# Dense chunks of 512 tokens, with columns 0-263 of the second product behind all logits and a list schedule for the front of the kernel

## The chip, the cores and the metric

One core of a Trainium2 chip runs the kernel. The engines are TensorE (PE, with its weight loads shown as PEld), VectorE (DVE), ScalarE (ACT), GpSimd (POOL) and SyncE (SP, which here only issues DMAs). The metric is device time in microseconds (us) of one launch, as the median of several runs.

## The reference

Three stages run one after another, all in float32 precision.

1. Sparse attention: q, k, v of 4 batches x 8 heads x 576 positions x 64. Heads 0 to 3 look at the last 32 positions, heads 4 to 7 at the earlier positions of the same residue class modulo 32:

```python
scores = np.where(masks[None], scale * q @ k.T, -1e9)
attn = exp(scores - max); attn = attn / (sum(attn) + 1e-09)
x = (attn @ v)                    # 2304 tokens x 512
```

2. A dense feed-forward: `h = x @ w_in` (512 to 2048), `g = h * sigmoid(h)`, `x = g @ w_out` (2048 to 512). These two weights come as 64-bit floats.

3. A mixture of 8 experts with a greedy global assignment: `logits = x @ w_gate`, all 18,432 logits sorted from the top, and each token goes to the first expert that still has one of its 288 places. Then `out[mask] = relu(x[mask] @ w1[e]) @ w2[e]` for each expert e (512 to 1024 to 512).

## The kernel before

**Arithmetic.** Every product of the dense and the expert stage is done as three fp32r matmuls: each operand is split into a high part (an ACT copy, rounded) and a low part (DVE: source minus high part), and high x high, high x low and low x high are summed in PSUM.

**Front.** `attention` works in pairs of heads, 16 in all, 4 for each batch; a pair has two halves with `scores` (PE, then DVE maximum, ACT exponentials), `norm` (DVE or POOL), `turn` (PE transposes, ACT copies), and then `values` (PE, ACT and DVE copies into the tile xf of the batch). The 64-bit weights arrive as raw words. `pieces` (lines 610, 613, 616) rebuilds float32 from them with three DVE operations for 512 elements, and its second part (lines 625, 626) splits them. `gate_turn` and `gate_columns` fold the router's `w_gate` into `w_out`: for every two blocks of w_out, 8 transposes (line 641), two ACT copies and 16 small matmuls (line 656) give 8 more columns, so that the second product delivers the logits too.

**Dense stage.** The tokens are 9 chunks of 256. A unit is a chunk and one of 8 pairs of 128-row blocks of the hidden layer. `gemm1` has 24 matmuls of 256 columns a unit (lines 693 to 695), `silu` two ACT and two DVE operations of 128x512. `gemm2` follows one unit behind. Its output columns are in two parts: A, columns 0-255 (line 746), and B, columns 256-511 with the 8 logits, 264 wide (line 749), each 12 matmuls a unit. Chunks 0 and 1 compute A and B at once; chunks 2 to 8 (`DEFER = 2`) compute B alone and store g, the high and low parts, to DRAM (tiles gd).

**Order.** The front is written out by hand: `START` names for each step of the first batch's attention what else is issued (C a conversion step, L a split, T and G gate steps, X a split of x, P a part of gemm1, R a load), and `BESIDE` does so for each half unit of chunks 0 and 1. A small list, `REST`, holds low parts back for a step. From the middle of chunk 1 on, `side` spreads the attention of batches 1 to 3 over the units of chunks 1 to 5. Engines run their queues in the order of issue; so does SP with its DMAs.

**Behind the logits.** `Router.phase` finds one expert's tokens at a time (DVE with small PE products). Meanwhile PE does the put-off A columns of chunks 2 to 8, with g read back into six buffers gk (`RELOADS`), the router's products in between by `tick` and `hop`, a running estimate of the time. Then x of the first expert is gathered, and 8 experts run in `ffn_a` and `ffn_b`, while the router goes on and the expert weights are loaded and split.

Of the kernel before, what the change touches and what calls it, by code (L numbers as in the profile page):

```python
# [23 lines left out]
NE = 8  # L24
# [21 lines left out]
DEFER = 2  # L46
RELOADS = 6

START = (
    "", "", "", "", "", "", "", "", "C0 C0 C1 C0 Rs2", "Ro1", "L0 C1 C1 C2", "C2", "L1 C2 C3", "C3 Ri3",
    "C3 L3", "", "", "L2", "X0 X2", "C4 X1", "C4 C4 C5 T1 C5 P10", "C6 L4 C5 P00 P11", "X3",
)
BESIDE = (
# [4 lines left out]
)  # L62
SPARE_SB = 2
FIRST_LOADS = "e q0 v0 q2 q1 i01 v2 o01 i00 o00 v1 i10 q3 v3 i11"
# [6 lines left out]
CLOSED = 1.0e6  # L71

# [291 lines left out]
def kernel(  # L364
# [22 lines left out]
    gdr = {(c, fp): dram.tile([128, 2, 512], F, name=f"gd{c}_{fp}") for c in range(DEFER, NCHUNK) for fp in range(NFP)  # L387
           if c <= LATE or fp < 2}
# [15 lines left out]
    xsp = pool(ctx, name="xsp", bufs=4, side="right")  # L404
    st_xf, st_bat, st_ps, st_c = (ctx.enter_context(ExitStack()) for _ in range(4))
# [3 lines left out]
    pacc = pool(st_ps, name="pacc", bufs=1, space=PSUM)  # L409
# [24 lines left out]

    REST = []

    def rest(what, f, src=False):
        REST.append([what, f, 0, src])

    def settle(what=None, src=False):  # L440

        for r in list(REST):
            if src and r[3] or what is not None and what == r[0] or (
                    what is None and not src and r[2] > 0):
                REST.remove(r)
                r[1]()
            else:
                r[2] += what is None and not src

    def new_sb():  # L450
        settle()
        if sum(r[3] for r in REST) > SPARE_SB:
            settle(src=True)
        return ap.tile([128, 512], F, name="sb", bufs=7)


    def scores(n, half):
        if half == 0 and NPAIR < n + 1 < NP:
            load_qk(n + 1)
# [23 lines left out]
        sb = new_sb()  # L483
# [8 lines left out]
        nc.vector.tensor_scalar(mx[:, :units], mx[:, :units], -1.0 / math.sqrt(D), None, op0=OP.mult)  # L492
        sm = ap.tile([128, 5], F, name="sm")
# [5 lines left out]
    def norm(n, half):  # L499
        sv, sm = PR[n, half]  # L500
        units = 5 if half == 0 else 4
        nc.vector.tensor_scalar(sm[:, :units], sm[:, :units], 1e-9, None, op0=OP.add)
        nc.vector.reciprocal(sm[:, :units], sm[:, :units])
        if (n, half) in NORM_ON_POOL:
            nc.gpsimd.tensor_tensor(sv, sv, sm[:, :units, None].to_broadcast([128, units, WIN[n % NPAIR]]), op=OP.mult)
        else:
            for u in range(units):
                nc.vector.tensor_scalar(sv[:, u, :], sv[:, u, :], sm[:, u:u + 1], None, op0=OP.mult)

    def turn(n, half):  # L510
# [3 lines left out]
        for u in range(4):  # L514
            nc.tensor.transpose(pt[:W, 128 * u:128 * u + 128], sv[:, u, :], ident)
        t = ap.tile([96, 512], F, name="ptA" if half == 0 else "ptB", bufs=1)
        nc.scalar.activation(t[:W], pt[:W], AF.Copy)
        PT[n, half] = t
        if half == 0:
            pt = patt.tile([128, 512], F, name="att")  # L520
            nc.tensor.transpose(pt[:W, :128], sv[:, 4, :], ident)
            t = ap.tile([96, 128], F, name="ptM", bufs=1)
            nc.scalar.activation(t[:W], pt[:W, :128], AF.Copy)
            PT[n, 2] = t

    def values(n):
        b, pr = divmod(n, NPAIR)
        W = WIN[pr]
        if pr == 0:
            XF[b] = xfp.tile([128, NPAIR, S], F, name="xf")  # L530
        x = XF[b][:, pr, :]
        v = VW.pop(n)
        av = patt.tile([128, 512], F, name="att")
        for j in range(8):
            for a in range(2):
                mm(av[64 * a:64 * a + 64, 64 * j:64 * j + 64], v[:W, j, 64 * a:64 * a + 64],
                   PT[n, a][:W, 64 * j:64 * j + 64], start=True, stop=True)
        if pr < 2:
            nc.scalar.activation(x[:, :512], av, AF.Copy)
        else:  # L540
            xs = x.rearrange("p (i r) -> p r i", r=STRIDE)
            nc.scalar.activation(xs[:, 0:28, :], av[:, :504].rearrange("p (r i) -> p r i", i=NCLS), AF.Copy)
            nc.vector.tensor_copy(xs[:, 28, 0:8], av[:, 504:512])
        av = patt.tile([128, 512], F, name="att")
        for a in range(2):
            mm(av[64 * a:64 * a + 64, 0:64], v[:W, 8, 64 * a:64 * a + 64],
               PT[n, 2][:W, 64 * a:64 * a + 64], start=True, stop=True)
        if pr < 2:
            nc.vector.tensor_copy(x[:, 512:576], av[:, :64])
        else:  # L550
            nc.vector.tensor_copy(xs[:, 28, 8:18], av[:, 0:10])
            nc.vector.tensor_copy(xs[:, 29:32, :], av[:, 10:64].rearrange("p (r i) -> p r i", i=NCLS))
        if NPAIR < n + 1 < NP:
            load_v(n + 1)

    def attention(n0, n1):

        for k in range(2 * n0, 2 * n1 + 3):
            if k < 2 * n1:
                scores(*divmod(k, 2))  # L560
                yield
            if k >= 2 * n0 + 4 and k % 2 == 0:
                values(k // 2 - 2)
                yield
            if 2 * n0 < k <= 2 * n1:
                norm(*divmod(k - 1, 2))
            if 2 * n0 + 2 <= k < 2 * n1 + 2:
                turn(*divmod(k - 2, 2))
# [3 lines left out]
    WI, WO, RAW, ST, WT2, LATER = {}, {}, {}, {}, {}, {}  # L572

    def alloc_w(kind, c):
        n, t = (512, "wa") if kind == "i" else (520, "wb")
        (WI if kind == "i" else WO)[c] = tuple(wpool.tile([128, 4, n], R, name=t) for _ in range(2))

    def load_raw(kind, c, h, tag):
# [4 lines left out]
        t = wpool.tile([128, 2, 1024], I32, name=tag)  # L583
        nc.sync.dma_start(t, src)
        for k in range(2):
            RAW[kind, c, 2 * h + k] = t[:, k].rearrange("p (f w) -> p f w", w=2)

    def load_spare(kind, c, p, t):
        if not wide:
            return  # L590
        t = t.bitcast(I32)[:, 0:1024]
        nc.sync.dma_start(t, (w_in if kind == "i" else w_out)[c, p].bitcast(I32))
        RAW[kind, c, p] = t.rearrange("p (f w) -> p f w", w=2)

    def pieces(kind, c, p):

        if kind == "i" and p == 0 and c:
            alloc_w("i", c)
        if kind == "o" and p == 0 and c:
            alloc_w("o", c)  # L600
        sts = [new_sb() for _ in range(2)]
        if not wide:
            for i in range(2):
                nc.sync.dma_start(sts[i], (w_in if kind == "i" else w_out)[c, p + i])
        else:
            r = [RAW.pop((kind, c, p + i)) for i in range(2)]
            d = [st.bitcast(I32) for st in sts]
            v = nc.vector
            for i in range(2):
                v.tensor_scalar(d[i], r[i][:, :, 1], 3, 0x3FFFFFFF, op0=OP.logical_shift_left, op1=OP.bitwise_and)  # L610
            yield
            for i in range(2):
                v.scalar_tensor_tensor(d[i], r[i][:, :, 1], -0x40000000, d[i], op0=OP.bitwise_and, op1=OP.bitwise_or)  # L613
            yield
            for i in range(2):
# [669 lines left out]
```

## Time and profile before

| | us |
|---|---|
| median of 3 runs | 851.85 (851.37 to 852.91) |
| the profiled execution | 850.23 |
| its span, first to last instruction | 848.5 |
| PE busy | 798.8 (94%) |
| DVE busy | 505.0 (60%) |
| ACT busy | 364.5 (43%) |
| POOL busy | 81.2 (10%) |
| PE's share of the chain that ended last | 76% |

The profile is of one execution. Busy time counts an instruction from start to end; matmuls are pipelined and overlap, so the pace of PE is read from the distance between starts and not from durations. PEclk is the clock that was granted to PE, as a share of 2.4 GHz. A DMA share of 1 means that all 16 DMA engines are busy.

### The profile page before, as it was taken

Reading aid. Unit: us, or ns where it says so; the run is one execution under the profiler, and the core shown is the slowest. Engines: PE = TensorE matmul, PEld = TensorE weight load, DVE = VectorE, ACT = ScalarE, POOL = GpSimd, SP = SyncE. Lnnn points to the kernel's source line nnn. Section 1 sums busy time; section 2 is a strip of 40 time slices with the busy share of each in tenths; the row PEclk is TensorE's granted clock in tenths of the full one; section 3 lists DMA queues with packets and bytes.
Section 4 is the critical chain, followed back from the end, with each engine's and each line's share of the span. In section 5 each row is a group of like instructions: output and inputs, shape, how many; then the busy total and the mean of one; then the engine's idle time right before and its main releaser. Section 6 shows DMA issues by size and latency. Waiting matters only on the chain.

```text
span 848.5 us, 19455 instructions
## 1 busy us (share of the span) xinstructions
PE 798.8 (94%) x7623; PEld 771.5 (91%) x7623; DVE 505.0 (60%) x1582; ACT 364.5 (43%) x933; POOL 81.2 (10%) x133
## 2 busy tenths in 40 slices
PE   4689889999999999999999998999999999999995
PEld 3579888999999999899999998899999999999995
DVE  2959965564554554433334377778787887874440
ACT  3454434554455544443323212102455465456541
POOL 0000000000000000000003000001120311133631
PEclk9999989999999999999999999999999999999998
DMA  9960231231444444323335279993555655565630
GB/s 325 362 246 1 77 110 34 78 109 55 171 150 155 152 146 142 129 105 137 131 131 195 91 229 344 372 324 121 158 171 161 183 159 170 153 184 163 212 108 28
DMA packets 56907, 137.32 MB, mean 162 GB/s; under 512 B 6768, under 2 KB 10352, under 8 KB 56816
## 3 DMA queue, kind: packets, MB, share of 16 engines
q1 hardware_dynamic: 48832, 121.39, 42.7%
q0 software_dynamic: 3232, 9.96, 3.8%
q10 hardware_dynamic: 4752, 4.73, 1.6%
q8 instruction: 59, 0.97, 0.5%
q14 instruction: 32, 0.26, 0.1%
HBM read 99.89 MB, written 36.18 MB: 160 GB/s over the span
## 4 chain that ended last, share of the span: by engine, by line
PE 76%; DVE 13%; DMA 4%; ACT 4%; issue 1%; POOL 1%; ACTq 0%; POOLq 0%; SPq 0%
PE accB L749 11%; PE ph L693 7%; PE ph L695 7%; PE ph L694 7%; PE accA L746 6%; PE pm L1116 4%; PE pm L1117 4%; PE pm L1118 4%; PE pm L1095 3%; PE pm L1096 3%; PE pm L1097 3%; PE ph L746 3%; DVE sb L613 2%; PE att L210 2%; PE att L477 2%; DVE sb L616 2%
## 5 line engine op out<-in xcount | busy, mean ns | idle before, releaser
L693 PE MATMUL ph<-xh,wa 128*128 128x256 f32 x576 | 166.9, 290 | 0.0
L695 PE MATMUL ph<-xh,wa 128*128 128x256 f32 x576 | 164.0, 285 | 2.5 <-DVE wa L626 2.5
L694 PE MATMUL ph<-xl,wa 128*128 128x256 f32 x576 | 163.8, 284 | 0.5 <-DVE xl L675 0.5
L749 PE MATMUL accB<-wb,g 128*128 128x264 f32 x792 | 133.5, 290 | 0.5 <-ACT x2e L768 0.4
L712 DVE SCALAR_TENSOR_TENSOR gf<-gf,ph 128x512 f32<-128x512 f32 x72 | 49.5, 687 | 125.8 <-ACT gf L711 125.5
L749 PEld LDWEIGHTS accB<-wb,g 128*128 128x128 f32 x792 | 114.8, 192 | 2.5 <-ACT x2e L768 1.5
L695 PEld LDWEIGHTS ph<-xh,wa 128*128 128x128 f32 x576 | 110.5, 192 | 2.7 <-DVE wa L626 2.7
L693 PEld LDWEIGHTS ph<-xh,wa 128*128 128x128 f32 x576 | 110.7, 192 | 1.5
L694 PEld LDWEIGHTS ph<-xl,wa 128*128 128x128 f32 x576 | 110.7, 192 | 0.8 <-DVE xl L675 0.8
L711 ACT ACTIVATE gf<-ph 128x512 f32<-128x512 f32 x72 | 42.7, 594 | 93.2 <-PE ph L695 83.4
L1116 PE MATMUL pm<-hh,wb 128*128 128x288 f32 x256 | 80.3, 314 | 0.0
L1095 PE MATMUL pm<-xh,wa 128*128 128x288 f32 x256 | 76.9, 301 | 0.0
L1096 PE MATMUL pm<-xl,wa 128*128 128x288 f32 x256 | 75.7, 296 | 0.6 <-DVE xl L1081 0.6
L1117 PE MATMUL pm<-hl,wb 128*128 128x288 f32 x256 | 75.6, 295 | 0.6 <-DVE hl L1102 0.6
L1097 PE MATMUL pm<-xh,wa 128*128 128x288 f32 x256 | 75.5, 295 | 0.0
L1118 PE MATMUL pm<-hh,wb 128*128 128x288 f32 x256 | 75.3, 294 | 0.0
L495 ACT ACTIVATE sb<-sb,mx 128x96 f32<-128x96 f32 (+1 forms) x108 | 38.5, 358 | 46.5 <-DVE mx L492 43.0
L399 DVE TENSOR_TENSOR g<-gf,g 128x512 fp32r<-128x512 f32 x50 | 34.6, 693 | 34.9 <-ACT g L398 34.9
L746 PE MATMUL accA<-wb,g 128*128 128x256 f32 x192 | 51.1, 300 | 3.2 <-DVE g L715 1.8
L1117 PEld LDWEIGHTS pm<-hl,wb 128*128 128x128 f32 x256 | 48.3, 189 | 0.8 <-DVE hl L1102 0.8
L1096 PEld LDWEIGHTS pm<-xl,wa 128*128 128x128 f32 x256 | 48.1, 188 | 0.8 <-DVE xl L1081 0.8
L1116 PEld LDWEIGHTS pm<-hh,wb 128*128 128x128 f32 x256 | 48.2, 188 | 0.0
(260 smaller groups left out, 1666.9 us busy)
## 6 DMA issues: line engine op xcount, KB each, us to landing
g<-in_w_dram SPq DMA_DIRECT2D x128, 256.0 KB, 3.0
gd<-g SPq DMA_DIRECT2D x100, 256.0 KB, 2.0
gk<-gd SPq DMA_DIRECT2D x50, 512.0 KB, 5.5
qk<-in_qk_dram SPq DMA_DIRECT2D x13, 672.0 KB, 4.3
wa<-in_w_in_dram SPq DMA_DIRECT2D x6, 1024.0 KB, 17.4
vw<-in_vw_dram SPq DMA_DIRECT2D x13, 432.0 KB, 3.8
wa<-in_w_out_dram SPq DMA_DIRECT2D x2, 1024.0 KB, 11.2
qk<-in_w_out_dram SPq DMA_DIRECT2D x4, 512.0 KB, 4.8
```

The source lines that it names most:

```text
L693: mm(o, whi[:, d, cs], xh, start=d == 0 and k == 0, stop=False, skip_group_check=True)
L694: mm(o, whi[:, d, cs], xl, start=False, stop=False, skip_group_check=True)
L695: mm(o, wlo[:, d, cs], xh, start=False, stop=d == 3, skip_group_check=True)
L712: nc.vector.scalar_tensor_tensor(t, t, 1.0, ph, op0=OP.add, op1=OP.mult)
L746: mm(ACC[c, "A"][:, 256 * m:256 * m + 256], g[:, ts], w[:, fi, 0:256], start=first and m == 0 and i == 0, stop=last and i == 2, skip_group ...
L749: mm(ACC[c, "B"][m], g[:, ts], w[:, fi, 256:520], start=first and i == 0, stop=last and i == 2)
L1095: mm(ps, whi[:, d, cs], xh, start=d == 0, stop=False)
L1096: mm(ps, whi[:, d, cs], xl, start=False, stop=False)
L1097: mm(ps, wlo[:, d, cs], xh, start=False, stop=d == 3)
L1116: mm(ps, whi[:, f % 4, cs], hh, start=f == 0, stop=False)
L1117: mm(ps, whi[:, f % 4, cs], hl, start=False, stop=False)
L1118: mm(ps, wlo[:, f % 4, cs], hh, start=False, stop=f == 7)
```

## The change

- The dense stage has 4 chunks of 512 tokens (`CW`, `NW`) and one of 256. In the wide chunks a unit is one block of 128 hidden rows, and gemm1 has 12 matmuls of 512 columns; the x parts are tiles of 4 x 512. gemm2's B has 4 token blocks a unit, two to a PSUM bank, in 3 banks.
- The second product's columns are cut at 264: A is columns 0-263, B columns 264-511 with the logits, 256 wide. A of every chunk runs behind all logits (`gemm2_late`), so g of all chunks but the end of the last one is stored and read back. Its weights are stored in float32 (`wad`) while the front runs, loaded at the end of the dense stage, and split there (`split_a`).
- `START`, `BESIDE` and `REST` go. Up to the end of the first chunk, every step of attention (batches 0 and 1), conversion, gate, x split, gemm1, silu and gemm2 is an operation of `Plan` with an engine, an estimated length, what it comes after, a due time and the buffers it takes and gives. `Plan.run` takes, again and again, the engine that can start something first, and on it the operation that is due first, and issues it. `scores`, `norm`, `turn`, `values`, `pieces`, `gate`, `split_x` and `silu` become generators with a `yield` between engines; `turn` and `values` now issue both of their PE steps ahead of the copies.
- Conversions are done 1024 elements at a time. The attention of batches 2 and 3 stands beside chunks 1 and 2 (`side` in `beside`).

```diff
-DEFER = 2
+CW, NW = 512, 4
+NA = 264
+NB = DM - NA
+PAIRS = (0, 1, 2, 3, 4, 5, 6, 7, 8, 9, 12, 13, 10, 11, 14, 15)
+AFTER_NS = {"PE": 300, "ACT": 200, "DVE": 150, "POOL": 200, "DMA": 1500, None: 0}
+FIRST_NS, LOADS_NS, PITCH_NS = 50000, 5500, 7000
...
-FIRST_LOADS = "e q0 v0 q2 q1 i01 v2 o01 i00 o00 v1 i10 q3 v3 i11"
+FIRST_LOADS = "q0 v0 q2 q1 i01 v2 o01 i00 o00 v1 i10 q3 v3 i11"
+LATER_LOADS = "o20 o10 o11 i20 i21 i30 i31 q4 v4 o21 o30 o31 q5 v5 q6 v6 q7 v7 q8 v8"
...
+    def run(self):
+        left = list(self.ops)
+        while left:
+            can = [(t, o["due"], i) for i, o in enumerate(left) for t in [self.ready(o)] if t is not None]
+            first = min(can)[0]
+            eng = left[min(can)[2]]["eng"]
+            i = min((d, t, i) for t, d, i in can if left[i]["eng"] == eng and t <= first + 50)[2]
+            o = left.pop(i)
+            t = self.ready(o)
...
+            if o["emit"]:
+                o["emit"]()
...
+    gdw = {(c, fp): dram.tile([128, 2, 2, 2, CT], F, name=f"gd{c}_{fp}") for c in range(NW) for fp in range(NFP)}
+    wad = [dram.tile([128, 8, NA], F, name=f"wad{j}") for j in range(2)]
...
-    pacc = pool(st_ps, name="pacc", bufs=1, space=PSUM)
+    pacc = pool(st_ps, name="pacc", bufs=3, space=PSUM)
...
+    def gemm1(c, u, ds=range(4)):
...
+        n, blocks = (CW, (u,)) if c < NW else (CT, (2 * u, 2 * u + 1))
         for d in ds:
+            for k, f in enumerate(blocks):
                 whi, wlo = WI[f // 4]
+                o = ph[:, n * k:n * k + n]
+                mm(o, whi[:, d, cs], xh[:, d], start=d == 0 and k == 0, stop=False, skip_group_check=True)
+                mm(o, whi[:, d, cs], xl[:, d], start=False, stop=False, skip_group_check=True)
+                mm(o, wlo[:, d, cs], xh[:, d], start=False, stop=d == 3, skip_group_check=True)
...
+        for k, g in enumerate((gh, gl)):
+            if c < NW:
+                nc.sync.dma_start(gdw[c, u // 2][:, :, k, u % 2, :], g.bitcast(F).rearrange("p (h t) -> p h t", h=2))
...
+    def attend(n, due, pitch):
...
+            a = add("PE", 1150 + 250 * early, nx, [LD[f"q{n}"], masked], t, [bank, "sb"], [qk_of] * half)
+            a = add("DVE", 170 + 120 * u + 115 * u * (not early), nx, [a], t, ["mx"], [] if early else [bank])
+            a = add("ACT", 360 * u, nx, [a], t, ["sm"], ([bank] if early else []) + ["mx"])
...
+    def due_of(u):
+        return FIRST_NS + PITCH_NS * u
...
+    def convert(m):
+        kind, c, p = order[m]
+        t = due_of(4 * c) - 8000 + 2000 * (p // 2) if kind == "i" else due_of(4 * c + p + 1) - 10000
...
+    XD = [attend(n, 10000 + 10000 * n, 5000) for n in range(NPAIR)]
+    loads(LATER_LOADS)
+    for m in PAIRS:
+        convert(m)
...
+    XD += [attend(n, FIRST_NS + 6000 + 23000 * (n - NPAIR), 11500) for n in range(NPAIR, 2 * NPAIR)]
...
+    plan.run()
...
+    def split_a(j, low, f):
...
+        if low:
+            nc.vector.tensor_tensor(WOA[j][1][fs], SA[j][fs], WOA[j][0].bitcast(F)[fs], op=OP.subtract)
+        else:
+            nc.scalar.activation(WOA[j][0][fs], SA[j][fs], AF.Copy)
...
+    def gemm2_late(c, fp, tick=None):
...
+                    mm(ACC[c][m][:, 0:NA], g[:, ts], w[:, f % 8, :], start=f == 0 and i == 0,
+                       stop=f == DFF // 128 - 1 and i == 2)
+                    if tick:
+                        tick(122)
...
+        if i == len(seq):
+            gemm2_late(0, 0)
+        gemm2(*seq[i - 1])
...
+    for f in (0, 2, 4, 6):
+        split_a(1, True, f)
...
+    at["dve"] = 2700
...
     for c, fp in late:
-        gemm2(c, fp, "A", tick)
+        if c or fp:
+            gemm2_late(c, fp, tick)
         if back:
             reload()
```

## Rows read from the trace of the kernel before

**Rows 1.** page, part 2: busy tenths in 40 slices of 21.2 us

```profile
PE   4689889999999999999999998999999999999995
...
DVE  2959965564554554433334377778787887874440
```

**Rows 2.** stage table: length, busy us (instructions) by engine, PEclk, DMA share, GB/s

```profile
0.00:59.70 59.70, 38.94 (x328) 30.34 (x329) 36.40 (x105) 27.41 (x104) 4.11 (x9) 1.00 0.91 332
59.70:146.70 87.00, 79.53 (x644) 77.65 (x643) 63.71 (x126) 38.08 (x86) 0.00 (x0) 0.90 0.16 53
146.70:213.20 66.50, 64.99 (x736) 61.75 (x737) 36.72 (x124) 35.99 (x132) 0.00 (x0) 1.00 0.26 82
213.20:386.30 173.10, 171.31 (x1741) 165.57 (x1742) 84.93 (x244) 83.62 (x244) 0.00 (x0) 1.00 0.42 143
386.30:488.50 102.20, 101.37 (x842) 100.95 (x841) 36.43 (x63) 34.39 (x62) 8.37 (x37) 1.00 0.37 137
488.50:591.20 102.70, 98.32 (x1168) 95.61 (x1167) 78.30 (x396) 15.29 (x30) 2.90 (x3) 1.00 0.81 281
591.20:849.00 257.80, 244.28 (x2179) 239.67 (x2177) 168.47 (x528) 129.69 (x281) 65.86 (x84) 0.99 0.52 155
```

**Rows 3.** timeline of PE, the first matmuls of the first dense product

```profile
60.08 0.41 PE L694 MATMUL ph<-xl,wa 128*128 128x256 f32 x1
60.30 0.41 PE L695 MATMUL ph<-xh,wa 128*128 128x256 f32 x1
```

**Rows 4.** timeline of PE, 440 to 444 us: start, length, line, operation

```profile
440.86 1.63 PE L749 MATMUL accB<-wb,g 128*128 128x264 f32 x12
442.33 0.29 PE L693 MATMUL ph<-xh,wa 128*128 128x256 f32 x1
...
443.89 0.28 PE L694 MATMUL ph<-xl,wa 128*128 128x256 f32 x1
```

**Rows 5.** timeline of PE in the expert stage, 690 to 693 us

```profile
690.12 0.29 PE L1095 MATMUL pm<-xh,wa 128*128 128x288 f32 x1
...
691.57 0.29 PE L1097 MATMUL pm<-xh,wa 128*128 128x288 f32 x1
```

**Rows 6.** stage table, 503.5 to 549.8: all, line 746 alone; timeline at the logits' end

```profile
503.50:549.80 46.30, 41.94 (x458) 40.24 (x457) 36.06 (x174) 8.73 (x16) 0.00 (x0) 1.00 0.98 349
...
503.50:549.80 46.30, 37.49 (x292) 35.12 (x291) 1.00 0.98 349
...
486.35 0.51 PE L749 MATMUL accB<-wb,wa 128*128 128x264 f32 x2 [0.61 <-ACT wa L398]
```

**Rows 7.** instruction groups of DVE, 0 to 146.7 us: conversion and splits

```profile
L613 DVE SCALAR_TENSOR_TENSOR sb<-wa,sb 128x512 int32<-128x512 int32 x16 | 10.8, 720 | 0.0
L616 DVE SCALAR_TENSOR_TENSOR sb<-wa,sb 128x512 int32<-128x512 int32 x16 | 10.3, 682 | 0.0
...
L626 DVE TENSOR_TENSOR wb<-sb,wb 128x512 fp32r<-128x512 f32 x16 | 10.1, 684 | 0.0
...
L610 DVE TENSOR_SCALAR sb<-wa 128x512 int32<-128x512 int32 x16 | 6.0, 418 | 0.0
```

**Rows 8.** stage table of the score matmuls alone (line 477), two stretches

```profile
59.70:213.20 153.50, 9.36 (x178) 7.38 (x180) 0.94 0.20 66
213.20:386.30 173.10, 10.59 (x208) 8.32 (x208) 1.00 0.42 143
```

**Rows 9.** chain that ended last, two pieces of a gate step: start, us, what

```profile
125.58 1.68 PE att L656 x16
127.26 0.93 PE att L641 x8
```

**Rows 10.** timeline of PE, scores of the fourth pair

```profile
33.19 1.36 PE L477 MATMUL ph<-wb 64*64 64x82 f32 x16 [1.13 <-DMA wb<-in_qk_dram]
```

**Rows 11.** instruction groups of DVE, 146.7 to 213.2 us: attention

```profile
L508 DVE TENSOR_SCALAR sb<-sb,sm 128x96 f32<-128x96 f32 (+1 forms) x43 | 8.5, 263 | 0.4
...
L489 DVE TENSOR_TENSOR sb<-att,maskt 128x480 f32<-128x480 f32 (+3 forms) x9 | 5.2, 583 | 7.9 <-PE att L477 4.8 <-PE att L482 3.1
```

More of the change, by code (lines that the diff above doesn't have):

```diff
@@ L431, in load_v @@
         VW[n] = v
[L435 to L454, printed above, removed]
     def scores(n, half):
-        if half == 0 and NPAIR < n + 1 < NP:
+        if half == 0 and 2 * NPAIR < n + 1 < NP:
             load_qk(n + 1)
@@ L723 @@
[L723 to L741 removed]
+        yield
@@ new lines, with masks_in, load, loads @@
+    add = plan.add
+    plan.free["DMA"] = LOADS_NS
+    def masks_in():
+        nc.vector.tensor_copy(identb, ident)
+        for t, u0, u1 in raw:
+            nc.vector.tensor_copy(maskt[:, u0:u1], t)
+    there = add("DMA", 1600, None)
+    masked = add("DVE", 1000, masks_in, [there])
+    LD, before = {}, None
+    def load(key, size, emit, pool):
+        nonlocal before
+        before = LD[key] = add("DMA", size * 1024 // BYTES_PER_NS, emit, [before, there], 0, [pool])
+    def loads(text):
+        for tok in text.split():
+            k, n = tok[0], tok[1:]
+            if k == "q":
+                load(tok, 672, lambda n=n: load_qk(int(n)), "wb" if 1 <= int(n) < NPAIR else "qk")
+            elif k == "v":
+                load(tok, 432, lambda n=n: load_v(int(n)), "wb" if 1 <= int(n) < NPAIR else "vw")
+            else:
+                tag = "xf" if tok == "o20" else "wa" if tok in ("i00", "i01", "o00", "o01", "i10", "i11", "i20", "i21") else "wb"
+                load(tok, 1024, lambda k=k, n=n, tag=tag: load_raw(k, int(n[0]), int(n[1]), tag), tag)
@@ new lines, in LD_POOL @@
+    def LD_POOL(key):
+        return "xf" if key == "o20" else "wa" if key in ("i00", "i01", "o00", "o01", "i10", "i11", "i20", "i21") else "wb"
+    XD = [attend(n, 10000 + 10000 * n, 5000) for n in range(NPAIR)]
+    loads(LATER_LOADS)
+    for m in PAIRS:
+        convert(m)
+    XL = []
+    for d in range(NPAIR):
+        g = split_x(0, d, d + 1)
+        nx = lambda g=g: next(g, None)
+        a = add("ACT", 600, nx, [XD[d]], FIRST_NS - 5000, ["wb"] * 2 if d == 0 else [])
+        if d == 0:
+            first_split = a
+        a["after"].append(first_split if d else None)
+        a["after"] = [x for x in a["after"] if x]
+        XL.append(add("DVE", 690, nx, [a], FIRST_NS - 5000))
@@ L855, in side @@
+    XD += [attend(n, FIRST_NS + 6000 + 23000 * (n - NPAIR), 11500) for n in range(NPAIR, 2 * NPAIR)]
+    a = None
+    for h in range(2):
+        g = split_x(1, 2 * h, 2 * h + 2)
+        nx = lambda g=g: next(g, None)
+        a = add("ACT", 1400, nx, XD + [a], FIRST_NS + 105000, [] if h else ["wb"] * 2)
+        add("DVE", 1400, nx, [a], FIRST_NS + 105000)
+    plan.run()
+    del raw, t
+    att = attention(2 * NPAIR, NP)
+    nstep = 0
     def side(n):
@@ L874 @@
+    SA = {}
     rt = None
[L875 removed]
+    for i in range(16, len(seq) + 1):
         if i < len(seq):
[L877 to L907 removed]
```

654 lines of the change are left out of this document (351 added, 303 removed), and 4 rows, old and new, of the table BESIDE.

## The prediction

> **What bounds the kernel now.** I read the page's 40 slices first, then the stage table, then single rows. The slices [rows 1], 21 us each, show TensorE (PE) at 9 tenths from 127 us on, but for two slices at 8 and the tail, and lower ahead of that; there VectorE (DVE) is the engine that is full (9 tenths in slices 2, 4 and 5). So late changes are worth what they take from or add to PE's own work, and early ones what they do to PE's waiting.
>
> The stage table [rows 2] is cut at the first matmul of the first dense product (59.7 us), at the end of the second product of chunk 0 (146.7), of chunk 1 (213.2), of chunk 5 (386.3), of chunk 8 with all logits (488.5), and at the end of the columns that had been put off (591.2). Up to 146.7 DVE is busy 100 of 147 us; PE's granted clock is 0.90 from 59.7 to 146.7, so it stands partly at the lower of its two levels: the matmuls of 256 columns that start at 60.08 and 60.30 us are 0.22 apart, which is 256 columns at 1.2 GHz [rows 3], those of a full stretch 0.12 [rows 4]. From 386.3 on nothing but the dense products runs, with PE busy 101.4 of 102.2 us.
>
> The unit prices of PE are distances between starts, not the durations, which overlap. From 442.33 to 443.89 us lie 13 steps of 256 columns: 0.120 us each. From 440.86 to 442.33 lie 12 steps of 264 columns: 0.1225 [rows 4]. From 690.12 to 691.57 lie 11 steps of 288: 0.1318 [rows 5]. At 2.4 GHz a column takes 0.417 ns, so each matmul costs its columns plus 12 to 13 ns.
>
> **The dense products at 512 columns.** No matmul of this type with 512 columns is in the trace. Above it cannot cost more than two of 256 (0.240); below, not less than its columns (0.213). The three rows have one slope and one rest, so I take 0.2133 + 0.0127 = 0.226. Four chunks of 16 units of 12 such matmuls are 768, each in place of two: 768 x (0.240 - 0.226) = 10.8 us less; with the ends of the range 0 and 20.7.
>
> The Trainium skill (TensorE: Matmul & The Clock Gate, Back-to-back issue gap) gives a gap of N/2.4 + 2.5 ns, an estimate of 0.216 us at 512. The rows carry about 12 ns and not 2.5 above the columns, so here the trace disagrees; by the rule the 768 matmuls would save 7.7 us more.
>
> **The second product's columns.** Columns 0-263 (A) and 264-511 with 8 logit columns (B) are now 264 and 256 wide instead of 256 and 264, and A of chunks 0 and 1 goes behind the logits too. As PE is full there, a moved matmul is paid again where it lands. What lands behind the logits: 72 units of 12 instead of 56. One fills the wait for the last activation (restart at 486.35 after 0.61 us of idling [rows 6]); 71 x 12 x 0.1225 = 104.4 against 56 x 12 x 0.120 = 80.6: +23.8 us. The stored g is read back 512 KB a unit (66 reads for 50). Of 503.5 to 549.8 us DMA was busy 0.98 at 349 GB/s and PE 41.9 of 46.3 us [rows 6]: 4.4 us lost. The stage carried 281 GB/s x 102.7 us = 28.9 MB [rows 2]; 16 more reads make 37.3 MB in some 129 us, 289 GB/s: as near the limit as before, for longer. I add 2 us (between 0, if the added units run while DMA is free, and 9, below). Sum of the stage: +26.
>
> A's weights are stored, loaded and split again: 8 ACT and 8 DVE operations of 528 elements. The nearest row is the 512-element split, 0.684 us [rows 7], so 5.5 us on DVE, beside dense work where DVE is busy 36 of 102 us and ACT 34 [rows 2]; at the router's start four of them delay it by under 3 us, which 100 us of waiting matmuls cover. Uncovered, that is +3; I take 0.
>
> **The dense stage between.** Before, 213.2 to 386.3 held four chunks of 192 x 0.120 + 96 x 0.1225 = 34.8 us and 208 score matmuls, 6.5 pairs at 32 a pair [rows 8]: (173.1 - 139.2)/6.5 = 5.2 us a pair, waits included. After: three chunks of 192 x 0.226 + 192 x 0.120 = 66.4, one of 34.6, less one first-product unit that lies ahead of the cut (2.7), and 8 pairs at 5.2 = 41.6: 272.7 us against 275.3 from 213.2 to 488.5: -2.6. The pairs now stand denser (8 in two chunks); 4.6 to 6.0 us a pair moves this by -5 to +6. The g stores have runs of 1 KB where they had 2; DMA is busy 0.37 there [rows 2], and four g buffers leave a store two units (over 8 us), so nothing is added.
>
> **The front stage, the largest term.** From 59.7 to 213.2 (153.5 us) PE had: 17 units of the first product (chunk 2's first among them) x 24 x 0.120 = 49.0; A 192 x 0.120 = 23.0; B 192 x 0.1225 = 23.5; 7 gate steps of 1.68 + 0.93 = 2.6 [rows 9], 18.2; 178 score matmuls, 5.6 pairs at 5.2 = 28.9 [rows 8]. That is 142.6, so 10.9 us were lost to waits and the lower clock. After, the same 512 tokens need 17 x 12 x 0.226 = 46.1; B at 192 x 0.120 = 23.0; 8 gate steps 20.8; 4 pairs 20.8: 110.7 us.
>
> When does it start? The fourth pair's scores wait for their load until 33.19 us [rows 10]; the load order there is the same. Then follow softmax, transposes and values. The old order puts a gate step and a part of the conversion ahead of 59.7; the plan gives the pairs earlier due times. Bounds 48 and 62; I take 54. For the loss I take 8 (bounds 0 and 25): DVE still has to convert 16 MB of 64-bit weights, 32 times 0.42 + 0.72 + 0.68 us for 512 elements by [rows 7], in double-width operations now, but beside twice the dense work per converted weight, and without the low parts of A's weights (about 5.6 us go later). The stage ends at 54 + 110.7 + 8 = 172.7 for 213.2: -40.5.
>
> What is issued there, loads, weight stores and g stores on SP's queue too, goes in the planner's order. A store that waits for DVE holds the loads behind it; after 60 us the DMA share was 0.16 [rows 2], so that room covers it; uncovered, one such wait costs a conversion's length, some 2 us, inside the 25.
>
> **Sum.** -40.5 - 2.6 + 26 = -17.1 us on the profiled execution's 850.23 (span 848.5): 833.1. The median shown is 851.85, 1.62 above it; so 835 us. The expert stage (257.8 us) keeps its work; router products that move ahead of it only change places.
>
> **Rivals.**
>
> 1. The planned order is worse than the written one (slower). The place is DVE's in-order queue up to the first chunk's end. DVE was busy 36.4 + 63.7 + 36.7 = 136.8 of 213.2 us, 64% [rows 2]. Its work after: 5.6 less for A, and 1.6 pairs less at 4 x 0.58 + 9 x 0.26 = 4.7 us [rows 11], 7.3: 124 us. If it gets no better share than 64%, because a mask addition or a split placed by estimated lengths waits on a late PE or ACT step and holds the conversions behind it, the stage ends at 194 and the time is 856. It decides from a stage end of 190, a share of 65%. For it: two engines near their limit, three transposition banks now shared by gate steps and attention, and a lower clock whenever PE waits. Against: from 64 to 106 us DVE was at 9 tenths in the old order too [rows 1]; its idle time lay after the conversions, where the new order puts more. Chance 0.16.
>
> The clock part of it is in the Trainium skill (same page, The HAM clock gate): an idle array falls to half its rate. The trace agrees [rows 3].
>
> 2. Nothing lost and a quick start: 48 + 110.7 + 2, 12 us less; 823, with the 512 columns at their lower bound 813. For it: PE's waits ahead of 146.7 are all for DVE, whose work shrinks and spreads. Against: in-order queues rarely leave 2 us of loss, and the slope of the widths [rows 4, 5]. Chance 0.17; the rule on the gap alone would give 827 and has 0.1 of this.
>
> 3. The put-off columns become bound by DMA. All 71 units at the pace of the saturated stretch, 292 matmuls, some 24 units, in 46.3 us [rows 6] = 1.93 each, are 137 us against 102.7: +34 instead of +26; 843. For it: the saturation is there; against: it comes where expert weights load too. Chance 0.1.
>
> 4. The change doesn't do what it says: estimated lengths miss, the first chunk's first matmul stays at 60 and the loss near 19, so what the width gives goes into the front; 852. Chance 0.05.
>
> **How the numbers follow.** The forecast, 835 with 825 to 845 of its own, has 0.52. Forecast, second and third rival are faster, 0.79; the fourth, within 0.2%, what this kernel's timing can tell from no change, 0.05; the first, slower, 0.16. The range: 817 leaves the second rival's lower end out, 853 most of the first.
>
> **What would show it.** Right: first dense products by 54 us, starts of 512-column matmuls 0.226 apart, logits done near 445, put-off columns near 129 us long, the clock at 1.0 after the start. Wrong: 0.240 a matmul (10 us less gain), the first chunk's end beyond 185, a long row of waits for the read-back. It fails if PE idles in the front stage more than it did.

## The result and the profile after

The changed kernel took 827.85 us (median of 4 runs, 826.6 to 831.37) against 851.61 us of the kernel before beside it: ratio 0.9727, 95% interval 0.9693 to 0.9761. Forecast were 835 us, so its direction and most of its size held, and 7 us more were gained. Two later measurements of the same program, on two chips, gave 0.983 (0.9793 to 0.9867) and 0.9779 (0.9734 to 0.9823): the gain is some 2 to 3 per cent.

The profiled execution has a span of 824.9 us for 848.5: 23.6 us less. Here are the slices of the page of the kernel after, 20.6 us each, that answer to [rows 1], with the granted clock:

```profile
PE   4979999898999999999999899999999999999995
...
DVE  2998896355555543433345866878787886544530
...
PEclk9979999999999999999999999999999999999998
```

PE is at 9 tenths from the fourth slice (62 us) on, nearly without a break; it was from 127 us. The stage table of the kernel after is cut at 54 us (the start that the prediction took for the dense work), at the ends of the second product of the four wide chunks and of the last, narrow one (all logits), and at the end of the put-off columns. Columns: length, busy us (instructions) of PE, PEld, DVE, ACT, POOL, then PEclk, DMA share, GB/s.

```profile
0.00:54.00 54.00, 36.11 (x355) 27.17 (x356) 38.21 (x89) 28.28 (x100) 5.00 (x9) 0.98 0.98 359
54.00:168.00 114.00, 109.58 (x910) 96.00 (x910) 84.43 (x172) 60.33 (x161) 0.00 (x0) 0.95 0.51 165
168.00:260.00 92.00, 88.38 (x753) 74.61 (x753) 49.51 (x138) 48.10 (x155) 0.00 (x0) 1.00 0.51 162
260.00:341.50 81.50, 81.21 (x648) 69.83 (x649) 39.26 (x106) 37.75 (x99) 0.00 (x0) 1.00 0.42 135
341.50:408.60 67.10, 67.10 (x399) 59.74 (x398) 23.47 (x36) 24.09 (x41) 8.37 (x37) 1.00 0.47 158
408.60:441.50 32.90, 32.90 (x276) 32.90 (x275) 13.12 (x22) 12.46 (x21) 0.00 (x0) 1.00 0.49 178
441.50:574.50 133.00, 127.16 (x1494) 123.78 (x1493) 100.32 (x503) 18.21 (x37) 2.88 (x3) 1.00 0.83 286
574.50:825.00 250.50, 239.47 (x2032) 236.08 (x2031) 146.76 (x408) 128.86 (x278) 86.90 (x100) 0.99 0.52 158
```

Beside [rows 2], stage by stage:

| | before | after | difference | forecast |
|---|---|---|---|---|
| to the first 512 tokens' end | 213.2 | 168.0 | -45.2 | -40.5 |
| to the end of the logits | 275.3 | 273.5 | -1.8 | -2.6 |
| put-off columns | 102.7 | 133.0 | +30.3 | +26 |
| expert stage, to the span's end | 257.3 | 250.4 | -6.9 | 0 |
| span | 848.5 | 824.9 | -23.6 | -17.1 |

The unit price of the wide matmul is read, as in [rows 4], from starts. Timeline of PE of the kernel after, in its fourth chunk (start, length, line, operation):

```profile
349.75 0.40 PE L725 MATMUL ph<-wb,wa 128*128 128x512 f32 x1
...
352.27 0.39 PE L727 MATMUL ph<-wb,wa 128*128 128x512 f32 x1
```

Eleven steps in 2.52 us are 0.229 each, for the 0.226 that was estimated.

The last two lines of the table hide an exchange. Here are the router's small matmuls alone, in the put-off and in the expert stage, first of the kernel before, then of the kernel after (length, busy us (instructions) of PE and PEld, PEclk, DMA share, GB/s):

```profile
488.50:591.20 102.70, 16.08 (x432) 13.80 (x432) 1.00 0.81 281
591.20:848.50 257.30, 11.88 (x324) 10.33 (x324) 0.99 0.52 155
```

```profile
441.50:574.50 133.00, 20.65 (x558) 17.36 (x558) 1.00 0.83 286
574.50:824.90 250.40, 7.18 (x198) 6.19 (x198) 0.99 0.52 158
```

As the put-off stage is longer, 126 more of these matmuls fit into it. That is 4.6 us of its +30.3, and 4.7 of the -6.9 behind it.

### The profile page after: what moved, and what is told of

Read it like the earlier page. It is cut to its first block, busy times and chain, and to the rows that moved or that the text cites. A ratio compares the mean times of both kernels' runs of the same rounds, so it can differ in the third digit from the quotient of the medians.

```text
span 824.9 us, 17916 instructions
## 1 busy us (share of the span) xinstructions
PE 781.9 (95%) x6855; PEld 720.1 (87%) x6855; DVE 495.1 (60%) x1471; ACT 358.1 (43%) x887; POOL 103.1 (13%) x149
## 4 chain that ended last, share of the span: by engine, by line
PE 78%; DVE 8%; DMA 6%; ACT 5%; issue 1%; SPq 0%; ACTq 0%; POOL 0%; POOLq 0%; DVEq 0%
PE acc L773 10%; PE ph L725 7%; PE ph L726 7%; PE ph L727 7%; PE acc L1012 6%; PE pm L1261 4%; PE pm L1262 4%; PE ph L1012 4%; PE pm L1263 4%; PE pm L1282 4%; PE pm L1283 4%; PE pm L1284 4%; PE att L256 2%; ACT sb L521 2%; DMA gk<-gd 2%; PE att L501 2%
## 5 line engine op out<-in xcount | busy, mean ns | idle before, releaser
L725 PE MATMUL ph<-wb,wa 128*128 128x512 f32 (+1 forms) x320 | 124.5, 389 | 6.5 <-ACT wb L708 6.1
L726 PE MATMUL ph<-wb,wa 128*128 128x512 f32 (+1 forms) x320 | 120.7, 377 | 2.2 <-DVE wb L711 2.2
L727 PE MATMUL ph<-wb,wa 128*128 128x512 f32 (+1 forms) x320 | 119.8, 374 | 0.0
L773 PE MATMUL acc<-wb,g 128*128 128x256 f32 x792 | 108.0, 286 | 0.0
L773 PEld LDWEIGHTS acc<-wb,g 128*128 128x128 f32 x792 | 101.3, 190 | 4.3
L725 PEld LDWEIGHTS ph<-wb,wa 128*128 128x128 f32 x320 | 61.6, 193 | 16.8 <-ACT wb L708 6.6
L727 PEld LDWEIGHTS ph<-wb,wa 128*128 128x128 f32 x320 | 61.5, 192 | 10.9
L726 PEld LDWEIGHTS ph<-wb,wa 128*128 128x128 f32 x320 | 61.8, 193 | 10.5 <-DVE wb L711 3.1
L748 DVE TENSOR_TENSOR g<-gf,g 128x512 fp32r<-128x512 f32 x66 | 45.6, 691 | 38.9 <-ACT g L746 38.9
L746 ACT ACTIVATE g<-gf 128x512 fp32r<-128x512 f32 x66 | 41.6, 631 | 43.8 <-DVE gf L744 43.8
L1012 PE MATMUL acc<-wb,gk 128*128 128x264 f32 x408 | 55.6, 289 | 4.3 <-DMA gk<-gd 4.3
L1012 PEld LDWEIGHTS acc<-wb,gk 128*128 128x128 f32 x408 | 51.2, 188 | 4.8 <-DMA gk<-gd 4.7
L1012 PE MATMUL ph<-wb,gk 128*128 128x264 f32 x384 | 52.2, 289 | 1.0 <-DMA gk<-gd 1.0
## 6 DMA issues: line engine op xcount, KB each, us to landing
wa<-in_w_in_dram SPq DMA_DIRECT2D x6, 1024.0 KB, 12.8
```

The lines of the kernel that those rows point to most:

```text
L725: mm(o, whi[:, d, cs], xh[:, d], start=d == 0 and k == 0, stop=False, skip_group_check=True)
L726: mm(o, whi[:, d, cs], xl[:, d], start=False, stop=False, skip_group_check=True)
L727: mm(o, wlo[:, d, cs], xh[:, d], start=False, stop=d == 3, skip_group_check=True)
L773: mm(ACC[c][m // 2][:, m % 2, :], g[:, ts], w[:, f % 8, :], start=first and m % 2 == 0 and i == 0, stop=last and i == 2, skip_group_check= ...
L1012: mm(ACC[c][m][:, 0:NA], g[:, ts], w[:, f % 8, :], start=f == 0 and i == 0, stop=f == DFF // 128 - 1 and i == 2)
```

## The experiments

The theory at the start: of the gain, some 9 us come from the 512-column matmuls, the put-off columns cost what they take behind the logits, and the rest comes from the front, where the wide first chunk and the plan give TensorE something to do while VectorE converts the weights. The rivals: VectorE still bounds the front; the planner's exact order makes the gain; the put-off alone does it. Below, the front is the time up to the end of the first 512 tokens.

**The changed kernel again**, as a measure for the three kernels that ran beside it (two with an edit of the changed kernel, one of the kernel before).

> The changed kernel itself, unaltered, as the yardstick for the others: 0.972 of the kernel before, as first measured (0.969 to 0.976).

Measured: 839.05 us, ratio 0.983, span 838.0. Of the 13.1 us more in the span, 4.9 are there by the first chunk's end, nearly all of it from the first 60 us (below, under the hardware). The rest, 8.3 us, is in the expert stage, 258.7 us for 250.4, around one stall. The timeline of PE of this run (in brackets the idle time ahead and who ended it):

```profile
688.87 0.16 PE L372 MATMUL att<-r,above 128*128 128x1 bf16 x1 [4.53 <-DVE r L397]
```

Behind it the granted clock is 0.76 from 690 to 700 us, so part of the other 3.8 us is PE at the lower clock. The two other kernels with this stage that ran on the same chip had the stall too (4.55 and 4.56 us), those on the two other chips did not. ACT stands still beside DVE (4.8 us), and for both the profile names nothing on this core that they wait for: the cause isn't known. So the kernels below are compared by stages, beside this run or the later repeat; four edits of the changed kernel (one operation left out, later due times, attention held back, half of g read back) ran on a third chip, without the unaltered changed kernel beside them. Where the front is unaltered, it ended at 168 and 171 us with an early beginning, and at 172.5, 172.9 and 176.9 with a late one (the last part tells the two apart): a difference of less than some 4 us in one profile of the front says nothing.

**Matmuls of 512 columns cut in two**, all else as changed:

```diff
-                o = ph[:, n * k:n * k + n]
-                mm(o, whi[:, d, cs], xh[:, d], start=d == 0 and k == 0, stop=False, skip_group_check=True)
+                for j in range(n // CT):
+                    o = ph[:, n * k + CT * j:n * k + CT * j + CT]
+                    xa, xb = xh[:, d, CT * j:CT * j + CT], xl[:, d, CT * j:CT * j + CT]
+                    mm(o, whi[:, d, cs], xa, start=d == 0 and k == 0 and j == 0, stop=False, skip_group_check=True)
...
```

> The changed kernel with each first-product matmul of 512 columns issued as two of 256, all else the same. Theory (TensorE's work is the bound from the first chunk on, 0.2285 us at 512 for 2 x 0.120): 768 x 0.0115 = +8.8 us over the changed kernel, about 837 us. Rival A (the front hides it, it counts in chunks 1 to 3 only): +6.6 us. Rival B (the width is hidden, the gain is all in the planned front): 0 to +2 us.

Measured: 845.96 us, ratio 0.9906 (0.9874 to 0.9938); 6.9 us over the repeat in time, 8.3 in span, spread over the four wide chunks (4.3, 1.3, 1.6, 2.1). By the starts, 768 x (0.240 - 0.229) = 8.4 us. Timeline of PE of this kernel, 6 steps in 0.72 us:

```profile
359.04 0.28 PE L727 MATMUL ph<-wb,wa 128*128 128x256 f32 x1
...
359.76 0.28 PE L727 MATMUL ph<-wb,wa 128*128 128x256 f32 x1
```

So the width is worth 7 to 9 us: a third of the gain as first measured (23.8 us), half of the 14.2 us that the repeat beside it shows. The rest has another source. Rival B is out; theory and rival A are too near to each other for this run to decide, since the 4.3 us of the first chunk are no more than unaltered fronts differ by.

**Put-off alone, in the kernel before:** A of chunks 0 and 1 goes behind the logits too, with 256-token chunks and the written order.

```diff
-DEFER = 2
+DEFER = 0
...
-            rest(("g", c, fp), lambda: nc.vector.tensor_tensor(gl, t, gh.bitcast(F), op=OP.subtract))
+            def low():
+                nc.vector.tensor_tensor(gl, t, gh.bitcast(F), op=OP.subtract)
+                for k, g in enumerate((gh, gl)):
+                    nc.sync.dma_start(gdr[c, fp][:, k], g.bitcast(F))
+
+            rest(("g", c, fp), low)
```

> The kernel before with one part of the change alone: columns 0-255 of chunks 0 and 1 put off behind the logits too (DEFER = 0), chunks still of 256, the written order kept. Theory (a moved matmul is paid again where it lands): logits 15 to 23 us sooner, 16 more units behind them for about 29 us with the router's products that move along, expert stage 7 us shorter; in all 0 to +9 us, ratio 1.000 to 1.011. Rival (earlier logits are the gain, since the router starts sooner): 10 us or more faster, ratio under 0.988.

Measured: 867.95 us, ratio 1.0183 (1.0147 to 1.022): slower, and by more than was expected. The stage table of this kernel for chunk 0, chunk 1 and the put-off columns:

```profile
59.50:144.10 84.60, 72.84 (x548) 70.90 (x548) 63.45 (x125) 36.43 (x79) 0.00 (x0) 0.86 0.29 98
144.10:204.00 59.90, 55.74 (x639) 51.98 (x639) 35.27 (x121) 35.79 (x133) 0.00 (x0) 0.97 0.49 161
...
480.90:611.80 130.90, 126.56 (x1525) 123.44 (x1524) 99.68 (x506) 18.64 (x37) 3.06 (x3) 1.00 0.84 291
```

The put-off stage grew by 28.2 us: 23 us are the matmuls that left the first two chunks, and 5.5 the router's, which came over from the expert stage (that is 2.7 us shorter). But chunk 0 is only 2.4 us shorter than in [rows 2] (84.6 for 87.0), and the logits are done 7.6 us earlier. What was taken out of chunk 0, 96 matmuls or 11.5 us, had run in time that PE would else have waited: the DVE column has not moved (63.45 for 63.71), PE's idle time rose from 7.5 to 11.8 us, and PEclk fell from 0.90 to 0.86. Chunk 1 gives only 6.6 us for its 11.5 as well (59.9 for 66.5). Most of that is again waiting, here for the low part of g (the longest wait of PE in chunk 1; line waited for: us, times, longest):

```profile
PE accB L755 <- DVE g L717: 3.2, 2, 3.0
```

By itself this part of the change is a loss of 15 us (867.95 for 853.23 of the kernel before beside it).

**Is it the conversion that chunk 0 waits for?** In the kernel before, PE is idle for 7.5 us from 59.7 to 146.7 us, all of it waiting for DVE, most of it for the lines that rebuild or split the weights (616, 626):

```profile
PE att L641 <- DVE sb L616: 2.7, 2, 1.5
PE ph L695 <- DVE wa L626: 2.5, 1, 2.5
PE accA L746 <- DVE wb L626: 1.4, 1, 1.4
...
```

The second of the three operations that rebuild a weight is left out (the weights and the output are then others), in the kernel before and in the kernel just told:

```diff
-            for i in range(2):
-                v.scalar_tensor_tensor(d[i], r[i][:, :, 1], -0x40000000, d[i], op0=OP.bitwise_and, op1=OP.bitwise_or)
             yield
```

> The kernel before with the second of the three operations that rebuild a float32 weight left out (32 operations of 0.72 us on VectorE less, 23 us, so the weights and the output are not the reference's). In the changed kernel the same omission gave nothing. Theory: the narrow chunks of the kernel before compute only half as much for each converted weight, so its front is bound by the conversion: chunk 0's end (146.7) comes 8 to 19 us earlier, the time falls by 6 to 15 us, to 836 to 845. Rival: the written order's fixed places and not VectorE's work hold TensorE up: 0 to 3 us.

> The kernel before with columns 0-255 of all chunks put off and the same operation of the conversion left out (output not the reference's). With the conversion whole, putting off cost 15 us: 23 us of products moved behind the logits, but the logits came only 7.7 us earlier. Theory: the front was waiting for the conversion, so what was moved out of it only turned into waiting; with less conversion the logits come 10 to 20 us earlier than 480.9, and the time falls by 9 to 18 us, to 850 to 859. Rival: the front waits for something else (loads, softmax steps, order): under 3 us, 865 or more.

Measured: 837.24 us, ratio 0.9838 (0.9799 to 0.9877), and 849.93 us, ratio 0.9969 (0.9942 to 0.9996). Their stage tables from the first dense product to the end of chunk 0, and chunk 1, first with A of these chunks in place, then with it put off:

```profile
55.80:132.00 76.20, 73.74 (x644) 72.31 (x642) 51.47 (x105) 37.96 (x86) 0.00 (x0) 0.95 0.18 61
132.00:198.50 66.50, 65.00 (x736) 61.76 (x736) 36.68 (x124) 36.00 (x132) 0.00 (x0) 1.00 0.26 82
```

```profile
55.60:131.70 76.10, 70.52 (x548) 68.79 (x548) 51.16 (x104) 36.37 (x79) 0.00 (x0) 0.89 0.33 111
131.70:192.60 60.90, 56.76 (x639) 53.00 (x639) 35.24 (x121) 35.76 (x133) 0.00 (x0) 0.94 0.48 158
```

With 81.4 us of work on DVE up to chunk 0's end, for 100.1 in [rows 2] (18.7 less, not the 23 that were expected), that end comes at 132.0 instead of 146.7, and from the first dense product on PE has the same 644 instructions there. The whole gain of the span (12.8 us) is in this place; chunk 1 takes 66.5 us as before. The 14.7 us are 3.9 of an earlier first dense product, 5.0 less idle time of PE (2.5 for 7.5) and 5.8 less busy time for the same instructions, at a granted clock of 0.95 for 0.90: with the shorter waits came a higher clock, and it gave more than the waits themselves. So chunk 0 of the kernel before was bound by the conversion: theory held, rival out. And even now, taking A out of chunk 0 moves its end only from 132.0 to 131.7. Chunk 1 with A put off is no shorter for the omission (60.9 for 59.9): what it loses there has another source than the conversion. The second kernel is 18 us under the one with put-off alone; 12.9 of them are there at the logits' end (468.0 for 480.9), the others in the expert stage and not explained. With less conversion the put-off still costs 12.7 us (849.93 for 837.24).

**The same omission in the changed kernel** (one operation of 1024 elements for two of 512):

```diff
         if wide:
-            v.scalar_tensor_tensor(d, r[:, :, 1], -0x40000000, d, op0=OP.bitwise_and, op1=OP.bitwise_or)
+            pass
```

> The changed kernel with the second of the three VectorE operations that rebuild the weights left out (sign and top exponent bit of each weight are lost; the number of operations elsewhere is the same): 16 x 1.2 = 19 us less VectorE time in the front, in the same order. Theory (106 us of TensorE work stand in the 114 us from 54 us to the first chunk's end, 8 lost): 3 to 8 us faster than the changed kernel. Rival (VectorE is the bound of the front): 15 us or more faster.

Measured: 832.34 us, ratio 0.9767 (0.9721 to 0.9813). The stage table of its front, and below it the dense part of the front of a kernel on the same chip whose front is unaltered (the one that reads half of g, below):

```profile
0.00:54.00 54.00, 40.19 (x350) 30.20 (x350) 27.74 (x76) 26.18 (x97) 5.00 (x9) 1.00 0.91 328
54.00:175.50 121.50, 115.13 (x915) 100.14 (x916) 77.82 (x170) 62.33 (x164) 0.00 (x0) 0.92 0.52 169
```

```profile
54.00:176.90 122.90, 115.22 (x915) 100.50 (x916) 89.74 (x180) 62.52 (x164) 0.00 (x0) 0.92 0.52 167
```

DVE has 105.6 us of work up to the end of the first 512 tokens, where the repeat has 123.2; yet that end is at 175.5, against 176.9 in the unaltered front beside it and 172.9 and 172.5 in two runs of the changed kernel on other chips, all with the late beginning. What gave 14.7 us at chunk 0's end before gives 1.4 us at most here, less than such fronts differ by. Neither the theory's 3 to 8 us nor the rival's 15 came; it settles that DVE no longer bounds the front. The waits agree. From 54 to 168 us the kernel after has PE idle for 4.4 us, 1.0 of them for DVE:

```profile
PE ph L725 <- ACT wb L708: 1.9, 1, 1.9
PE att L501 <- DMA qk<-in_qk_dram: 1.5, 2, 1.0
PE ph L726 <- DVE wb L711: 0.6, 1, 0.6
PE ph L725 <- DVE gf L744: 0.4, 1, 0.4
```

The width of DVE's operations doesn't matter there either:

**Conversion in operations of 512 elements, as before:**

```diff
-        if wide:
-            v.tensor_scalar(d, r[:, :, 1], 3, 0x3FFFFFFF, op0=OP.logical_shift_left, op1=OP.bitwise_and)
+        hs = (slice(0, 512), slice(512, 1024)) if wide else ()
+        for h in hs:
+            v.tensor_scalar(d[:, h], r[:, h, 1], 3, 0x3FFFFFFF, op0=OP.logical_shift_left, op1=OP.bitwise_and)
...
```

> The changed kernel with the weights' rebuilding on VectorE in pieces of 512 elements as before, not 1024: 48 more instructions, some 0.06 us each, 3 us more VectorE time in the front. Theory (the front is bound by TensorE's work, with about 8 us of 114 lost): 0 to +1.5 us. Rival (VectorE bounds the front): +3 us or more.

Measured: 839.84 us, ratio 0.9841 (0.9809 to 0.9874); first 512 tokens done at 173.4 for 172.9. Both are within the theory's 0 to 1.5 us.

**Does the planner's order make it?** Two changes of it: due times of the units 9 us apart for 7, and the second batch's attention held back until the last conversion is through.

```diff
-FIRST_NS, LOADS_NS, PITCH_NS = 50000, 5500, 7000
+FIRST_NS, LOADS_NS, PITCH_NS = 50000, 5500, 9000
```

> The changed kernel with the planner's due times of the dense units 9 us apart in place of 7 (the second batch's attention keeps its due times and so goes ahead of conversions and gate steps). Theory (the order is one of many that keep TensorE full, since an operation that is ready goes when its engine is free): -2 to +5 us. Rival (the due times make the gain): +10 us or more.

```diff
-nx, [LD[f"q{n}"], masked], t, [bank, "sb"]
+nx, [LD[f"q{n}"], masked] + ([] if early else [SPLIT["o", 3, 2]]), t, [bank, "sb"]
```

> The changed kernel with one part of its planned order undone: the attention of batch 1 may begin only when the last weight conversion is done, as in the kernel before; the planner orders all the rest as it did. Theory (the front gains because attention, gate steps and conversion fill each other's waits): TensorE has about 21 us less to do while conversion runs and four pairs to do behind it, end of the first chunk 10 to 20 us later, in all +8 to +20 us over the changed kernel. Rival (the planned order itself is worth little, the wide chunks are): 0 to +3 us.

Measured: 835.99 us, ratio 0.9832 (0.9784 to 0.988), the first 512 tokens done at 168.5; and 833.96 us, ratio 0.9802 (0.9755 to 0.9849), done at 175.4, where 8 us at least had been expected by the theory; the rival's 0 to 3 us came. The first edit did what its theory said (168.5 for 168.0, both with the early beginning). The second took hold: here are the score matmuls of its front (line 501; length, busy us (instructions) of PE and PEld, PEclk, DMA share, GB/s).

```profile
54.00:115.00 61.00, 0.00 (x0) 0.00 (x0) 0.94 0.65 213
115.00:175.40 60.40, 7.17 (x144) 6.00 (x144) 0.94 0.41 125
```

The kernel after has 96 of these 144 ahead of 115 us, and its last split of a weight ends at 135.8 us, here at 115.5. So the conversion can end 20 us earlier or later and attention can stand beside it or behind it: neither moves the front by more than 3 us beside a run with the same beginning. The plan's fine order is not where the gain is. Not tried: narrow chunks under the planner, so what a good order gives apart from the wide chunk stays open.

**What the read-back costs behind the logits.** Only the high part of g is read back and used for both (output changed):

```diff
-            nc.sync.dma_start(g.bitcast(F).rearrange("p a (k t) -> p a k t", k=2), gdw[c // 2, fp][:, c % 2])
+            nc.sync.dma_start(g[:, 0].bitcast(F).rearrange("p (k t) -> p k t", k=2), gdw[c // 2, fp][:, c % 2, 0])
...
```

> The changed kernel reading back only the high part of g, 256 KB a unit in place of 512, and using it for the low part too; matmuls and their order are the same. Theory (TensorE is idle 5.8 of 133 us behind the logits, nearly all of it on these reads): 4 to 7 us faster than the changed kernel. Rival A (DMA bounds the whole stage): 10 us or more faster. Rival B (the reads are hidden): 0 to 1 us.

Measured: 828.4 us, ratio 0.9741 (0.9701 to 0.9781). The stage table for its put-off columns:

```profile
450.60:580.00 129.40, 126.55 (x1494) 123.72 (x1493) 100.34 (x503) 18.21 (x37) 2.88 (x3) 1.00 0.56 173
```

129.4 us for 133.0, with the DMA share down from 0.83 to 0.56: half of the read-back cost this stage 3.6 us, just under the theory's 4; 1.8 us of waiting for reads are left. Both rivals are out. In the kernel after, the waits of PE in it name them (line waited for: us, times, longest):

```profile
PE acc L1012 <- DMA gk<-gd: 4.3, 2, 2.9
PE ph L1012 <- DMA gk<-gd: 1.0, 1, 1.0
```

**A try to win these back.** The waits lie where the first expert's weights are loaded too, so their splits, and with them all loads but the first four, wait until the sixth narrow chunk. Beside it ran the changed kernel once more.

```diff
-    at["limit"] = 8
+    at["limit"] = 0
     hop()
     for c, fp in late:
+        if (c, fp) == (5, 0):
+            at["limit"] = 8
```

> The changed kernel with the first expert's weight pieces split, and so loaded, only from the put-off columns of the sixth narrow chunk on (4 of 16 are still loaded at the start, 12 move behind some 500 us). Theory: the put-off stage loses 5.8 us because weight pieces and read-back share the DMA between 470 and 500 us (share 0.99, PE 24.5 of 30 us); 8 pieces of 256 KB less there are 2.1 MB, 6 us of transfer at 348 GB/s; the stage falls from 133 to 128 to 131, the time by 2 to 5 us. Rival: the DMA is full of read-back alone, or the late pieces take the cover from the expert stage; the stage gives up to 1 us, or the expert stage takes it back: no change, or up to 3 us slower.

> The changed kernel once more, unaltered, as the measure for the kernel with the late weight pieces, and to see which of the two beginnings it shows (first two units of the first product done by 44.6 and 54.8 us, or by 49.7 and 59.2). Expected 827 to 840 us, a ratio of 0.973 to 0.984 to the kernel before, the put-off stage 132 to 134 us long.

Measured: 836.45 us, ratio 0.9833 (0.9792 to 0.9873), against 832.17 us, ratio 0.9779 (0.9734 to 0.9823). The intervals overlap, and no gain is to be seen. Put-off stage and expert stage of the kernel with late loads, then of the repeat:

```profile
444.40:577.90 133.50, 128.17 (x1475) 124.41 (x1474) 98.08 (x496) 17.44 (x36) 2.88 (x3) 0.99 0.82 283
577.90:830.00 252.10, 239.91 (x2051) 236.40 (x2049) 149.94 (x417) 129.44 (x280) 83.29 (x98) 0.99 0.53 158
```

```profile
446.10:579.70 133.60, 127.44 (x1494) 123.91 (x1494) 100.40 (x503) 18.30 (x37) 2.88 (x3) 1.00 0.82 285
579.70:829.90 250.20, 239.33 (x2032) 235.92 (x2030) 144.93 (x408) 128.97 (x278) 87.11 (x100) 0.99 0.52 158
```

The stage is as long as it was, with 19 PE instructions fewer in it, and these come in the expert stage. PE's waits for the reads did fall, to 3.1 us from the repeat's 5.5, and the stage is no shorter for it. Theory missed: the DMA share of the whole stage has not changed, the loads only lie elsewhere.

## Why the prediction was right, and where its sizes were off

- **The view it started from.** Early changes are worth what they do to PE's waiting, late ones what they add to PE's work: both halves were seen alone. A of chunks 0 and 1 costs 25.5 us behind the logits (28.2 in the put-off stage, 2.7 of it given back by the expert stage) and gives back 7.6 ahead of them when nothing else is changed. The forecast did not need that split: its front term was worked out for all parts together.
- **The 512-column matmul.** 0.226 was taken, 0.229 measured; the term was 10.8 us and is 8.4 by starts, 6.9 to 8.3 by the kernel with halves. The Trainium skill (TensorE: Matmul & The Clock Gate, Back-to-back issue gap) would make it 0.216; the trace disagrees, 16 ns above the columns and not 2.5. The second rival's lower end, which needed the columns alone (0.213), is out.
- **The front, -45.2 for -40.5.** The step that was mis-sized is "when does it start?". I let the whole 110.7 us of work begin at 54. The first matmul of the dense product starts at 32.68 us (its row stands in the last part), among the fourth pair's steps, and two of the sixteen units are done at 54.8. From 54 on, 105 us of work were left (110.7 less 2 x 12 x 0.226) and took 114: some 9 us more, for the 8 assumed. Of these 4.4 are PE's idle time, and half a pair of scores more than forecast (144 score matmuls for 128) lies here too; PEclk is 0.95. In the two repeats these units end 5 us later (49.7 and 59.2, 49.5 and 59.2, for 44.6 and 54.8), and the front ends at 172.9 and 172.5, the 172.7 of the forecast. That these two hit it is in part luck, since the term rests on a start that no run has.
- **The first rival** needed a DVE share of 64% and decided below 65%. Its work was sized rightly (124 us; 38.2 + 84.4 = 122.6 measured), the share is 122.6 of 168, 73%, and with 18 us of this work left out the front ends 1.4 us earlier at most. The rival was right on which engine held the front before; in the new front PE's waits for DVE are 1.0 us, so DVE's share decides nothing there.
- **The dense stage between:** 273.5 us for 272.7. Its terms held, each to 2 us: the chunk without attention took 67.1 for 66.4, and the attention of the two chunks before it, 242 score matmuls or 7.6 pairs for the 8 assumed, 5.2 us a pair as forecast.
- **The put-off stage, +30.3 for +26, and the expert stage, -6.9 for 0.** That router matmuls "only change places" was said and then not carried into the two stages: 4.6 us of them moved ahead. Without these the first is +25.7. The rest of the second, 2.2 us, is idle time of PE that is not there any more. Together they are +23.4 for +26.
- **The third rival** (bound by DMA, +34) is refuted: with the reads halved and 33% less DMA share only 3.6 us come back, and of the +30.3 the router's matmuls are 4.6.
- **Two readings that were off** without moving a term: [rows 1] has one slice at 8 tenths behind 127 us, not two, and the DMA share of 0.37 belongs to 386.3 to 488.5 us; from 213.2 to 386.3, where the stores were placed, [rows 2] has 0.42.

What is shown, then: the gain is no sum of parts that each help. The put-off loses 15 us in the old front: of the 23 us that it takes out of chunks 0 and 1 only 9 shorten them, in chunk 0 because what it takes out had covered the conversion, in chunk 1 because of another wait, which was read from the profile and not tested. In the new front the first chunk computes 512 tokens for each converted weight, and the conversion is off the path: the omission that gives 14.7 us at chunk 0's end in the old front gives 1.4 at most. The 7 to 9 us of the width come on top. That the cover is the wide chunk's and not the planner's is argued from the two changes of the order, and not shown: no run has narrow chunks under the planner.

## What to carry to other kernels

Before work is moved off a stage, see whether the engine that does it is the one the stage waits for: where it is not, the stage keeps its length and the work is paid again where it lands. Leave out a part of the suspected engine's work, in the old kernel and in the new one: the same omission then tells which of them it bounds. When work changes its stage, add it to the stage that gets it as well as taking it from the other.

## What the runs showed of the hardware

The same program begins in two ways. Timelines of PE, first of the kernel after, then of its second repeat:

```profile
32.68 0.80 PE L725 MATMUL ph<-wb,wa 128*128 128x512 f32 x1
33.28 0.63 PE L726 MATMUL ph<-wb,wa 128*128 128x512 f32 x1
33.70 0.63 PE L727 MATMUL ph<-wb,wa 128*128 128x512 f32 x1
...
39.03 0.39 PE L726 MATMUL ph<-wb,wa 128*128 128x512 f32 x1
39.26 0.39 PE L727 MATMUL ph<-wb,wa 128*128 128x512 f32 x1
```

```profile
33.44 0.63 PE L726 MATMUL ph<-wb,wa 128*128 128x512 f32 x1
33.86 0.63 PE L727 MATMUL ph<-wb,wa 128*128 128x512 f32 x1
...
48.44 0.63 PE L726 MATMUL ph<-wb,wa 128*128 128x512 f32 x1
48.86 0.63 PE L727 MATMUL ph<-wb,wa 128*128 128x512 f32 x1
```

512 columns take 0.42 to 0.43 us here, which is their number at 1.2 GHz, the lower level. In the first run the step is 0.23 from 39 us on, in the second it is still 0.42 at 48 us; the steps of attention stretch likewise, and the front is 4.5 us later at its end. Up to 34 us PE does the same steps in both, 0.16 us apart; what decides isn't known. The granted clock of the table shows 1.00 for both in 34.5 to 46 us, and in the second run also where its last two rows stand:

```profile
46.00:50.00 4.00, 4.00 (x12) 3.16 (x13) 3.90 (x10) 1.48 (x8) 0.00 (x0) 1.00 0.90 357
```

So at the start of a run the steps tell the level and the column does not.

The other surprise is the stall of 4.5 us in the expert stage: all three kernels with this stage showed it on one chip, and none on two others.
